# Fold weights of a routed expert layer: half of each expert's contraction computed before the routing is known

## The chip, the cores and the metric

One NeuronCore of a Trainium2 chip runs the whole program. The time is that of one execution on the device, in microseconds. Where several executions were timed, their median is given, with the lowest and the highest.

## The reference

Three layers follow one another on 3072 tokens of 512 features, all in float32.

```
state = gamma * state + k_t v_t^T ;  y_t = scale * q_t state        # 8 heads, 4 x 768 steps
e = argmax(y @ w_gate);  x = gate * eom * (relu(y @ w1[e]) @ w2[e])  # 8 experts, F = 1024
logits = x @ phi                                                    # 32 slots, 4 for each of 8 experts
d = softmax(logits, over tokens);  slot_in = d.T @ x
slot_out = relu(slot_in @ v1[e]) @ v2[e]
out = softmax(logits, over slots) @ slot_out
```

The scores of the second layer need x only through `x @ phi`. So the kernel doesn't form `relu(..) @ w2 @ phi` in that order: it folds `w2[e] @ phi` (1024 x 32) once for each expert and multiplies the hidden values by that.

## The kernel before

**Attention.** 24 steps of 128 tokens, in a loop over i with the steps' order written out by hand (`ORDER`, and `ORDER_22`, `ORDER_23`, `ORDER_24` for the last ones; each word is a function of the table `step`). One 1 MB tile `raw` per step (0.75 MB for the last of each six) holds q, k and v. It is loaded on SP's queue six steps ahead into a pool of seven buffers. Every third step, `x_put` (line 610) writes the tokens of three steps to `xs` in DRAM with four transfers on SP, and `scale_put` (line 602) their scales.

**Routing.** After the last step TensorE makes the gate logits (`gate_mm`, `gate_sum`), VectorE the choice, and TensorE the counts (line 659). VectorE works out the order in which the experts are taken (`ordi`), which depends on the counts. SP then reads the first expert's number and loads its weights. `rank` and 48 small matmuls (line 686, two for each step) make the lists of tokens per expert, and GpSimd gathers the first expert's tokens from `xs` (line 704). Then every engine passes a branch (line 818) round a part for experts with too many tokens, which isn't taken with these inputs.

**Experts.** Eight experts, each with up to 448 tokens, in order of their counts, eight units of 128 hidden features each. Unit g = 8e + f makes its hidden values with 12 matmuls (`l1`, line 883, weights split into two parts by ScalarE and VectorE, `split_w`). The pieces of the expert before (`behind`) run behind the units: scores, soft maxima, slot sums. A written order places them all, and each engine takes its instructions in that order.

**The fold.** `wq_load` loads a quarter of an expert's folded matrix (512 KB, the quarters are the units q of phi), `wq_mm` makes 16 matmuls of 128x256 (four for each q, into four groups of 32 partitions; each is two records in the profile), and `wq_turn` turns the result for use as weights in `logits`. Expert 0's four quarters are loaded as two 1 MB transfers in the routing (line 679), multiplied behind the list matmuls, and turned at line 718, ahead of the branch. For expert e + 1 the fold runs in expert e, at unit 2 (unit 4 in expert 0), and the quarters of expert e + 2 are loaded behind it.

**The last stage.** The slots go through the last experts (`moe2` weights, 32 MB in 128 tiles of 256 KB). `load_m2` loads 42 of these tiles into a pool of their own during the expert loop, and others into buffers that the loop no longer uses.

## Time and profile before

| | |
|---|---|
| median of 3 runs | 437.55 us (435.31 to 442.07) |
| the profiled execution | 435.42 us, its span 433.6 us |
| TensorE, VectorE, ScalarE, GpSimd busy | 87%, 60%, 37%, 25% of the span |
| TensorE's granted clock, mean | 0.948 of full speed |
| moved by DMA | 130.88 MB, 302 GB/s over the span |

The span runs from the first instruction of the profile to the last; the execution's time is 1.8 us longer. Attention takes the span to about 108 us, the routing to about 138, the eight experts to about 376, and the last stage the rest. Busy shares over the whole span mix these stages.

### The profile page before, as it was taken

How to read it: one execution, taken by the hardware profiler on the slowest of the kernel's cores; microseconds unless marked ns; L12 is line 12 of the kernel's file. 1: busy time of each engine (PE TensorE's matmuls, PEld its weight loads, DVE VectorE, ACT ScalarE, POOL GpSimd, SP SyncE). 2: the span in 40 equal slices, each digit the busy share in tenths (PEclk: the TensorE clock that was granted, in tenths of full speed). 3: DMA queues.
4: the chain of work that ended last, by engine and by line, in shares of the span. 5: the costliest groups of instructions: out<-in, count | busy, mean ns of one | idle time of the engine just before them, and what ended most of it. 6: DMA issues, size and time to landing. Idle time of an engine off the chain costs nothing.

```text
span 433.6 us, 11468 instructions
## 1 busy us (share of the span) xinstructions
PE 377.8 (87%) x4398; PEld 285.2 (66%) x4398; DVE 258.4 (60%) x676; ACT 162.2 (37%) x359; POOL 108.1 (25%) x117
## 2 busy tenths in 40 slices
PE   2989999998335999999999999999999996799990
PEld 2877777786214897778777867877778873224560
DVE  1498889998604365595574765754766756424350
ACT  1432222222012644655454644635454431112242
POOL 2303333321120413143052241421521212020020
PEclk9999999999655999999999999999999999699996
DMA  8999999963587798988978979889577789999998
GB/s 268 381 425 347 288 322 322 324 162 76 119 304 247 238 360 300 381 273 295 390 248 303 380 267 346 298 275 377 166 253 278 257 281 289 390 384 408 397 365 291
DMA packets 66275, 130.88 MB, mean 302 GB/s; under 512 B 10436, under 2 KB 28866, under 8 KB 63650
## 3 DMA queue, kind: packets, MB, share of 16 engines
q1 hardware_dynamic: 59426, 118.07, 78.4%
q0 software_dynamic: 3344, 8.34, 6.3%
q10 hardware_dynamic: 3440, 3.63, 2.5%
q8 instruction: 37, 0.61, 0.6%
q14 instruction: 28, 0.23, 0.2%
HBM read 116.84 MB, written 13.20 MB: 300 GB/s over the span
## 4 chain that ended last, share of the span: by engine, by line
PE 72%; DVE 9%; DMA 7%; issue 4%; ACT 3%; another core or an unknown queue 2%; SPq 1%; ACTq 1%; POOL 0%; DVEq 0%; POOLq 0%
PE hps L883 31%; PE s L414 5%; PE gps L992 5%; PE o L447 4%; PE fh L1176 4%; PE so L1213 3%; PE wps L241 3%; DMA raw<-in_qt_dram 3%; DMA xg<-xs,xidx 3%; PE lps L909 3%; PE xps L861 2%; PE o L438 2%; PE slo L1014 2%; PE st L461 1%
## 5 line engine op out<-in xcount | busy, mean ns | idle before, releaser
L883 PE MATMUL hps<-xh,wh 128*128 128x416 f32 (+2 forms) x256 | 92.0, 360 | 0.1
L883 PE MATMUL hps<-xl,wh 128*128 128x416 f32 (+2 forms) x256 | 88.9, 347 | 0.0
L883 PE MATMUL hps<-xh,wl 128*128 128x416 f32 (+2 forms) x256 | 88.7, 346 | 0.0
L222 DVE TENSOR_TENSOR wl<-r,wh 128x512 fp32r<-128x512 f32 x64 | 43.3, 677 | 43.6 <-ACT wh L221 41.2
L888 ACT ACTIVATE h<-hps 128x416 f32<-128x416 f32 (+2 forms) x64 | 32.7, 511 | 81.6 <-PE hps L883 75.9
L883 PEld LDWEIGHTS hps<-xh,wh 128*128 128x128 f32 x256 | 48.1, 188 | 15.1 <-issue 11.4
L975 POOL DMA_INDIRECT ctok<-ce,xidx x29 | 29.2, 1009 | 99.9 <-DVE ce L972 93.5
L221 ACT ACTIVATE wh<-r 128x512 fp32r<-128x512 f32 x64 | 40.0, 628 | 26.4 <-DMA r<-in_moe_w_dram 13.4
L883 PEld LDWEIGHTS hps<-xl,wh 128*128 128x128 f32 x256 | 48.2, 188 | 0.9 <-DVE xl L871 0.3
L883 PEld LDWEIGHTS hps<-xh,wl 128*128 128x128 f32 x256 | 48.1, 188 | 0.6
L704 POOL DMA_INDIRECT xg<-xs,xidx x29 | 29.9, 1031 | 65.3 <-ACT h L888 42.1
L424 DVE TENSOR_TENSOR sS<-s,csa 128x512 f32<-128x512 f32 x48 | 30.5, 675 | 16.3 <-PE s L414 16.3
L414 PE MATMUL s<-raw 64*128 64x128 f32 x384 | 32.5, 305 | 8.7 <-DMA raw<-in_qt_dram 8.3
L414 PEld LDWEIGHTS s<-raw 64*128 64x128 f32 x384 | 27.1, 204 | 11.5 <-DMA raw<-in_qt_dram 5.5
L895 DVE STREAM_TRANSPOSE hB<-h 128x416 f32<-128x416 f32 (+2 forms) x64 | 34.4, 576 | 0.0
L447 PE MATMUL o<-sS,raw 128*64 128x128 f32 x384 | 27.5, 288 | 0.0
L396 POOL TENSOR_TENSOR k<-raw,cs 128x512 f32<-128x512 f32 x20 | 22.3, 1132 | 17.0 <-DMA raw<-in_qt_dram 14.7
L479 ACT COPY xT<-o 128x512 f32<-128x512 f32 x24 | 13.9, 580 | 32.9 <-PE o L447 32.9
L241 PE MATMUL wps<-wt,phi 128*32 128x256 f32 x256 | 17.4, 414 | 9.0 <-DMA wt<-in_moe_w_dram 7.2
L447 PEld LDWEIGHTS o<-sS,raw 128*64 128x64 f32 x384 | 21.6, 142 | 3.9 <-issue 3.6
L992 PE MATMUL gps<-hB,pd 32*32 32x256 f32 x816 | 20.1, 405 | 3.7 <-DVE pd L946 3.7
L870 ACT ACTIVATE xh<-xps 128x416 fp32r<-128x416 f32 (+2 forms) x32 | 16.0, 513 | 14.8 <-DMA wt<-in_moe_w_dram 8.4
(174 smaller groups left out, 525.2 us busy)
## 6 DMA issues: line engine op xcount, KB each, us to landing
m<-in_moe_w_dram SPq DMA_DIRECT2D x41, 512.0 KB
r<-in_moe_w_dram SPq DMA_DIRECT2D x64, 256.0 KB
w<-in_moe_w_dram SPq DMA_DIRECT2D x64, 256.0 KB
wt<-in_moe_w_dram SPq DMA_DIRECT2D x28, 512.0 KB
m<-in_moe_w_dram SPq DMA_DIRECT2D x36, 256.0 KB
xs<-xr SPq DMA_DIRECT2D x32, 192.0 KB
raw<-in_kt_dram SPq DMA_DIRECT2D x5, 1024.0 KB
raw<-in_kn_dram SPq DMA_DIRECT2D x5, 1024.0 KB
```

Of the source, the lines that this page charges most:

```text
L221: nc.scalar.activation(out=hi, in_=t, func=ACTF.Copy)
L222: nc.vector.tensor_tensor(out=lo, in0=t, in1=hi, op=ALU.subtract)
L241: nc.tensor.matmul(out=wacc[k][32 * g:32 * g + 32, :], lhsT=phi[:, q, :], rhs=t, start=(q == 0), stop=(q == KD - 1), skip_group_check=True)
L414: nc.tensor.matmul(out=ps[h][:, p, :], lhsT=kq(i, p, 0)[r], rhs=kq(i, p, 1)[r], start=True, stop=True, tile_position=(64 * h, 0), skip_gro ...
L424: nc.vector.tensor_tensor(out=sS[i][:, h], in0=sps.pop((i, h)), in1=con("dm", 128)[:, 4 * h:4 * h + 4, :], op=ALU.mult)
L447: nc.tensor.matmul(out=o_at(i, p, h), lhsT=vals(i, 2 * p + h), rhs=s[:, h, p, :], start=(i % NCH == 0 and n < 4), stop=True, skip_group_ch ...
L704: gets.setdefault(e, []).append(nc.gpsimd.indirect_dma_start(out=t[0:r, :], out_offset=None, in_=xs[:, :], in_offset=bass.IndirectOffsetOn ...
L883: nc.tensor.matmul(out=ps, lhsT=a[:, kk * 128:(kk + 1) * 128], rhs=x[e][kk][:, 0:c], start=(n == 0), stop=(n == 11))
L888: relu.append(nc.scalar.activation(out=hs[g][:, 0:c], in_=ps, func=ACTF.Relu))
L895: nc.vector.transpose(out=hB[e][:, 0:NB[e], f, :], in_=hs[e * KF + f][:, 0:c].rearrange("p (b t) -> p b t", t=32))
L975: put = nc.gpsimd.indirect_dma_start(out=ctok[:, :], out_offset=bass.IndirectOffsetOnAxis(ap=xidx[0:r, e, j:j + 1], axis=0), in_=cn[0:r, j ...
L992: nc.tensor.matmul(out=ps[a][32 * j:32 * j + 32, :], lhsT=pd[q, b, :], rhs=hB[e][q, b].rearrange("p f t -> p (f t)"), start=(i == 0), stop ...
```

## The change

The contraction over the 512 features is cut in two. The units q = 0 and 1 of **all** experts, in the experts' own numbering, are loaded in the last eight steps of the attention loop (`first_load`, 1 MB each, into the pool of the attention tiles, which gets an eighth buffer). Their matmuls (`first_mm`, eight for each expert) stand in the last steps' order (P0 to P3) and between the list matmuls (4 to 7). ScalarE copies each result to SBUF (`first_copy`, four buffers), and SP stores it in a new DRAM tensor `wps` (`first_put`, 128 KB each).

The units q = 2 and 3 are still loaded by the experts' order, multiplied in the expert loop, and now for expert 0 too (at its unit 2). VectorE adds the stored half (`wq_add`), which SP has loaded by the expert's number (`part_load`), and `wq_turn` follows, for expert e at unit 1 of expert e itself (unit 2 in expert 0). Expert 1's second half is multiplied at unit 6 of expert 0, the others' at unit 3 of the expert before. The pool of the fold's quarters has two buffers in place of four, and 46 moe2 tiles in place of 42 are loaded into their own pool, with four in place of eight in the quarters' pool.

```diff
--- before.py
+++ after.py
@@ -34,15 +34,15 @@
 DX = DM + 16
 CX, NBX = max(C), max(NB)
 CAP = NT + 256
-NPRE, NX = 42, 4
+NPRE, NX = 46, 4
 NH = 6
-IO, UMM = 6, 2
+IO, UMM, QA = 6, 2, 2
 GROUPS = [(t, 3) for t in range(0, NTILE, 3)]
 ENDS = {t + n - 1: (t, n) for t, n in GROUPS}
 ORDER = "xe sc s m g1 gc xr rr g2 G0 Gb q oq os st G1 rk k".split()
 ORDER_22 = "xe sc s m st q oq os xr rr".split()
-ORDER_23 = "sc xe oq os rk3 xr".split()
-ORDER_24 = "xe g1 gc xr g2 G0".split()
+ORDER_23 = "sc xe oq os P0 rk3 xr".split()
+ORDER_24 = "xe g1 P1 C0 gc C1 xr g2 P2 P3 G0 C2".split()
 DH = (slice(0, 256), slice(256, 512))
 ORDC = "p 00 01 02 03 t 04 05 06 07 c s 10 11 o0-4 12 o4-8 13 o8-12 14 15 o12-16 16 17 d o16-20 S o20-24".split()
 QS = ((lambda nc: nc.sync, lambda nc: nc.scalar, lambda nc: nc.gpsimd), (lambda nc: nc.sync, lambda nc: nc.scalar))
@@ -165,6 +165,7 @@
 
     xs = dr.tile([NT + 1, DX], F32, name="xs")
     ctok = dr.tile([NT, NS], F32, name="ctok")
+    wps = dr.tile([E, 128, 256], F32, name="wps")
     inv = dr.tile([E * CAP, 1], I32, name="inv")
 
     phi = cst.tile([128, KD, NS], F32, name="phi")
@@ -225,7 +226,8 @@
 
 
 
-    wtt, wacc, wp = {}, {}, {}
+
+    wtt, wacc, wp, parts = {}, {}, {}, {}
 
     def wq_load(k, q, n, pool, tag):
         t = pool.tile([128, n * FF], F32, tag=tag, name="wt")
@@ -236,14 +238,17 @@
 
     def wq_mm(k, pool, tag):
         wacc[k] = pool.tile([128, 256], F32, tag=tag, name="wps")
-        for q in range(KD):
+        for q in range(QA, KD):
             for g, t in enumerate(wtt.pop((k, q))):
                 nc.tensor.matmul(out=wacc[k][32 * g:32 * g + 32, :], lhsT=phi[:, q, :], rhs=t,
-                                 start=(q == 0), stop=(q == KD - 1), skip_group_check=True)
+                                 start=(q == QA), stop=(q == KD - 1), skip_group_check=True)
+
+    def wq_add(k):
+        nc.vector.tensor_tensor(out=parts[k], in0=wacc.pop(k), in1=parts[k], op=ALU.add)
 
     def wq_turn(k, out):
         wp[k] = out
-        nc.vector.transpose(out=out, in_=wacc.pop(k).rearrange("p (f t) -> p f t", t=32))
+        nc.vector.transpose(out=out, in_=parts.pop(k).rearrange("p (f t) -> p f t", t=32))
 
 
 
@@ -311,7 +316,7 @@
 
     with ExitStack() as pa:
         sc2 = pa.enter_context(tc.tile_pool(name="sc2", bufs=2))
-        io = pa.enter_context(tc.tile_pool(name="io", bufs=IO + 1))
+        io = pa.enter_context(tc.tile_pool(name="io", bufs=IO + 2))
         one = pa.enter_context(tc.tile_pool(name="one", bufs=1))
         pT = pa.enter_context(tc.tile_pool(name="pT", bufs=1, space=PSUM))
 
@@ -381,6 +386,30 @@
                     r = slice(r.start, min(r.stop, 3 * DM))
                 nc.sync.dma_start(out=raw[i][:, r], in_=data[b][c][:, r])
 
+        ft, facc, fsum = {}, {}, {}
+
+        def first_load(e):
+            if 0 <= e < E:
+                ft[e] = io.tile([128, 4 * DM], F32, tag="raw", name="wt2")
+                nc.sync.dma_start(out=ft[e], in_=moe_w2[1, e, :, 0:QA * FF])
+
+        def first_mm(e):
+            t = ft.pop(e)
+            facc[e] = pT.tile([128, 256], F32, tag="st" if e % 2 else "w", name="fps")
+            for q in range(QA):
+                for g in range(4):
+                    nc.tensor.matmul(out=facc[e][32 * g:32 * g + 32, :], lhsT=phi[:, q, :],
+                                     rhs=t[:, q * FF + g * 256:q * FF + g * 256 + 256],
+                                     start=(q == 0), stop=(q == QA - 1), skip_group_check=True)
+
+        def first_copy(e):
+            fsum[e] = sc2.tile([128, 256], F32, tag="ws", name="ws", bufs=4)
+            nc.scalar.copy(out=fsum[e], in_=facc.pop(e))
+
+        def first_put(*es):
+            for e in es:
+                nc.sync.dma_start(out=wps[e], in_=fsum.pop(e))
+
         def kq(i, p, which):
             o = (p // 2) * DM + which * 256 + (p % 2) * 128
             return raw[i][:, o:o + 128]
@@ -620,6 +649,7 @@
             "g2": lambda i: gate_sum(i - 1), "G0": lambda i: gate_pick(i - 1), "Gb": lambda i: gate_own(i - 1),
             "G1": lambda i: gate_scale(i - 1),
             "oq": out_state, "q": lambda i: q_scale(i + 1), "os": out_scores, "st": state,
+            **{f"P{e}": lambda i, e=e: first_mm(e) for e in range(E)}, **{f"C{e}": lambda i, e=e: first_copy(e) for e in range(E)},
             "rk": lambda i: rank(i - 2), "k": lambda i: k_scale(i + 2),
         }
 
@@ -639,6 +669,7 @@
             if i < NTILE:
                 x_put(i - 3)
                 scale_put(i - 3)
+            first_load(i + IO + 1 - NTILE)
             for n in {NTILE - 2: ORDER_22, NTILE - 1: ORDER_23, NTILE: ORDER_24}.get(i, ORDER):
                 step[n](i)
             decay_table(i + 2)
@@ -651,6 +682,8 @@
         i = NTILE - 1
         x_put(i)
         gate_own(i)
+        first_copy(3)
+        first_put(0, 1, 2, 3)
         cp = pT.tile([128, 512], F32, tag="s", name="cp", bufs=2)
         key, counts = cp[:, 0:E], cp[:, E:2 * E]
         for o, w, b, first, final in ((key, eights, base[:, 0, 0:E], True, False), (key, ones, base[:, 1, 0:E], False, False),
@@ -676,15 +709,19 @@
         load_er(0)
         for g in range(3):
             load_w(g)
-        for q in range(0, KD, 2):
-            wq_load(0, q, 2, io, "raw")
         rank(i)
         lp = pT.tile([128, 32], F32, tag="s", name="lp", bufs=2)
         nc.tensor.matmul(out=lp, lhsT=ones, rhs=base[:, 2, :], start=True, stop=False)
         for u in range(NTILE):
             for a in range(2):
                 nc.tensor.matmul(out=lp, lhsT=lrow[:, u, :], rhs=lcol[:, u, a, :], start=False, stop=(a == 1 and u == NTILE - 1))
-        wq_mm(0, pT, "w")
+            if u == NTILE - 4:
+                for e in (4, 5, 6):
+                    first_mm(e)
+                    first_copy(e)
+        first_mm(7)
+        first_copy(7)
+        first_put(4, 5, 6, 7)
         lx = one.tile([128, E, 4, E], F32, name="lx")
 
         def lists(r):
@@ -715,7 +752,6 @@
         nc.vector.tensor_reduce(out=lim[:, E:E + 1], in_=lim[:, 0:E], axis=AX.X, op=ALU.max)
         nc.vector.tensor_copy(out=limi, in_=lim)
         lists(slice(1, E))
-        wq_turn(0, pd[:, 0:KF, :])
 
     whl = ctx.enter_context(tc.tile_pool(name="whl", bufs=3))
 
@@ -836,7 +872,7 @@
     hp = ctx.enter_context(tc.tile_pool(name="hp", bufs=NH))
     hbp = ctx.enter_context(tc.tile_pool(name="hbp", bufs=1))
     w2p = ctx.enter_context(tc.tile_pool(name="w2p", bufs=8))
-    wup = ctx.enter_context(tc.tile_pool(name="wup", bufs=KD))
+    wup = ctx.enter_context(tc.tile_pool(name="wup", bufs=KD - QA))
     with ExitStack() as pb:
         sp = pb.enter_context(tc.tile_pool(name="sp", bufs=1))
         ps_h = pb.enter_context(tc.tile_pool(name="ps_h", bufs=2, space=PSUM))
@@ -893,6 +929,10 @@
             if f == 0:
                 hB[e] = hbp.tile([128, NBX, KF, 32], F32, tag="hB", name="hB")
             nc.vector.transpose(out=hB[e][:, 0:NB[e], f, :], in_=hs[e * KF + f][:, 0:c].rearrange("p (b t) -> p b t", t=32))
+
+        def part_load(k):
+            parts[k] = sp.tile([128, 256], F32, tag="wpp", name="wpp")
+            nc.sync.dma_start(out=parts[k], in_=wps[bass.ds(er[k], 1)].rearrange("o p n -> (o p) n"))
 
         def load_w2(e, fs, pool=w2p, tag="w2"):
             for f in fs:
@@ -1046,11 +1086,12 @@
                 load_w2(e, (2 * f - 6, 2 * f - 5))
 
         load_er(1)
-        for q in range(KD):
-
-            get = wq_load(1, q, 1, wup, "wu")
-            if q == 0:
+        for q in range(QA, KD):
+
+            get = wq_load(0, q, 1, wup, "wu")
+            if q == QA:
                 after(get, gets[0])
+        part_load(0)
         for j in range(len(XT[0])):
             if j == 1:
                 split_w(0)
@@ -1091,15 +1132,25 @@
             else:
                 l1(g)
             behind(e - 1, f)
-            u = UMM if e else UMM + 2
-            if f == u and e + 1 < E:
-                wq_mm(e + 1, ps_1, "A")
-                wq_turn(e + 1, sp.tile([128, KF, NS], F32, tag="wp", name="wp", bufs=2))
-            if f > u and f <= u + 3 and e + 2 < E:
-
-                for q in ((0, 1), (2,), (3,))[f - u - 1]:
+
+
+            if g == UMM:
+                wq_mm(0, ps_1, "A")
+                wq_add(0)
+            if f == (1 if e else UMM):
+                wq_turn(e, sp.tile([128, KF, NS], F32, tag="wp", name="wp"))
+            if e + 1 < E:
+                if f == (2 if e else 3):
+                    part_load(e + 1)
+                if e == 0 and f in (3, 4):
+                    wq_load(1, QA + f - 3, 1, wup, "wu")
+                if f == (3 if e else 6):
+                    wq_mm(e + 1, ps_1, "A")
+                    wq_add(e + 1)
+            if e + 2 < E and f in ((4, 5) if e else (7,)):
+                for q in (QA + f - 4,) if e else range(QA, KD):
                     wq_load(e + 2, q, 1, wup, "wu")
-            elif G - 14 < g < G - 6 and f % 2:
+            elif g in (G - 12, G - 11):
                 load_m2(wup, "wu", 2)
             if g == G - 6:
                 load_w2(e, range(4), xp, "xy")
```

## Rows read from the trace of the kernel before

**Rows 1.** The page, chain that ended last, shares of the span by line.

```profile
PE hps L883 31%; PE s L414 5%; PE gps L992 5%; PE o L447 4%; PE fh L1176 4%; PE so L1213 3%; PE wps L241 3%; DMA raw<-in_qt_dram 3%; DMA xg<-xs,xidx 3%; PE lps L909 3%; PE xps L861 2%; PE o L438 2%; PE slo L1014 2%; PE st L461 1%
```

**Rows 2.** Busy time in two expert periods: stretch, engines, PEclk, DMA share, GB/s.

```profile
198.96:228.92 29.96, 29.66 (x303) 23.16 (x306) 19.00 (x44) 15.02 (x31) 9.68 (x9) 1.00 0.91 315
228.92:258.82 29.90, 29.55 (x294) 23.07 (x298) 18.87 (x44) 14.98 (x31) 9.67 (x9) 1.00 0.88 314
```

**Rows 3.** The chain in order of time: start us, us, what.

```profile
118.24 11.44 DMA xg<-xs,xidx
...
138.16 11.22 PE hps L883 x60
149.38 1.86 PE wps L241 x32
...
230.78 4.68 PE hps L883 x24
...
318.20 1.86 PE wps L241 x32
```

**Rows 4.** Timeline, attention's end and routing: start us, us, engine, line, operation.

```profile
79.86 1.09 PE L447 MATMUL o<-sS,raw 128*64 128x128 f32 x16
...
100.29 1.09 PE L447 MATMUL o<-sS,raw 128*64 128x128 f32 x16
...
103.72 0.37 ACT L467 COPY sts<-st 128x256 f32<-128x256 f32 x1 [0.92 <-PE st L461]
...
106.53 1.09 PE L447 MATMUL o<-sS,raw 128*64 128x128 f32 x16
...
108.31 0.85 PE L497 MATMUL g<-xT,wg 128*32 128x384 f32 x8 [0.68 <-ACT xT L479]
109.03 2.60 SPq L610 DMA_DIRECT2D xs<-xr  x4
...
109.76 0.84 PE L512 MATMUL g<-csa,gsb 128*128 128x16 f32 x6 [0.60 <-ACT gsb L505]
...
112.39 0.17 PE L659 MATMUL cp<-run,eights 128*128 128x8 bf16 x1 [1.75 <-DVE run L538]
...
116.89 0.60 PE L686 MATMUL lp<-lcol,lrow 128*128 128x32 bf16 x6 [2.93 <-DVE lrow L595]
...
118.24 1.27 POOL L704 DMA_INDIRECT xg<-xs,xidx  x1 [1.10 <-DVE sq L711]
...
121.16 1.01 POOL L704 DMA_INDIRECT xg<-xs,xidx  x1 [0.30 <-issue]
...
125.91 0.63 ACT L221 ACTIVATE wh<-r 128x512 fp32r<-128x512 f32 x1 [13.03 <-POOLq L818]
...
128.38 1.94 PE L241 MATMUL wps<-wt,phi 128*32 128x256 f32 x16 [1.72 <-SPq L818]
...
130.38 0.45 DVE L246 STREAM_TRANSPOSE pd<-wps 128x256 f32<-128x256 f32 x1 [10.58 <-PE wps L241]
...
134.56 0.49 DVE L852 TENSOR_SCALAR xg<-xg 128x512 f32<-128x512 f32 x1 [3.72 <-DVEq L818]
...
135.30 2.79 PE L861 MATMUL xps<-cs,xg 128*128 128x128 f32 x12 [4.99 <-DVE xg L852]
```

**Rows 5.** Busy time in the attention loop and in short stretches of the routing.

```profile
40.00:50.00 10.00, 9.36 (x182) 8.18 (x182) 9.54 (x30) 2.93 (x8) 3.40 (x4) 1.00 0.97 320
...
94.00:96.00 2.00, 2.00 (x50) 1.72 (x48) 1.93 (x6) 0.15 (x1) 1.16 (x3) 1.00 0.03 8
110.00:112.00 2.00, 0.64 (x8) 0.57 (x8) 1.08 (x7) 0.22 (x1) 0.00 (x0) 0.93 0.92 171
112.00:114.00 2.00, 1.57 (x52) 1.46 (x51) 1.76 (x10) 0.20 (x1) 0.00 (x0) 0.50 0.93 216
122.00:124.00 2.00, 0.00 (x0) 0.00 (x0) 0.00 (x0) 0.00 (x0) 0.17 (x1) 0.50 1.02 421
```

**Rows 6.** Busy time in the last stage.

```profile
396.00:420.00 24.00, 23.01 (x318) 14.33 (x319) 10.08 (x32) 7.47 (x18) 2.26 (x3) 1.00 1.04 391
```

## The prediction

> **What bounds the kernel now.** I read the chain of waits first, then the busy time stage by stage, then the routing stretch instruction by instruction, and last the transfers in two-microsecond windows. The chain by line [rows 1] puts 31% of the span on the expert layer's matmuls and 3% on the fold matmuls (`wps`, moe_w2 times phi). In the expert loop TensorE has no slack: 29.66 of 29.96 us busy in one expert, 29.55 of 29.90 in the next [rows 2]. What leaves TensorE's program there leaves the time. An expert's fold is 32 records in 1.86 us on the chain, and the chain has seven of them, from 149.38 to 318.20 [rows 3].
>
> The routing stretch, from the last attention step (107.6) to the first expert matmul (138.16), is bound by waits. The token gather is issued at 118.24 and the chain gives it 11.44 us [rows 3], beside 2.75 MB that SP issues around it (lines 677 to 680). But the gather isn't what ends last. The two 1 MB fold loads make the fold's second half run at 128.38; VectorE is held by its transpose until 130.38 + 0.45; only then does VectorE pass the branch of line 818, which costs 3.72 us, and scale the gathered rows at 134.56; the transposes run at 135.30 and the first expert matmul at 138.16 [rows 3, 4]. ScalarE had passed at 125.91, 3.74 us after GpSimd's third gather issue ended (121.16 + 1.01) [rows 4].
>
> **The loop's sum.** Before: 7 folds x 1.86 = 13.0 us of TensorE on the chain (expert 0's is in the routing). After: eight half folds in the loop, 16 records each, 0.93, so 7.4. Gain 5.6. Each half needs one VectorE add of 128x256 out of PSUM. No row shows such an add; the transpose of the same PSUM tile, 0.45 us [rows 4], is nearest, and I take that. Its bounds are nothing (hidden under the next unit of expert matmuls, 4.68 us for two [rows 3]) and 8 x 0.45 = 3.6 exposed. It is hidden for experts 2 to 7, where a whole unit of expert matmuls lies between the fold and the next user of PSUM tag A. It is not for expert 1: its fold stands at the end of unit 6 of expert 0, and the next thing on TensorE is the transposes of expert 1 into the same tag. That costs 0.45 plus the hand-over, 0.6 once. The 128 KB part loads queue on SP behind a VectorE transpose of the step before; the weight loads behind them have two units (4 us) in hand, so I price them at nothing; if that cover failed, a unit's start would slip by the transfer. The loop moves 5 MB less (7 MB of fold weights out, 1 MB of parts and 1 MB more of moe2 in), so DMA, at 0.88 to 0.91 there [rows 2], doesn't become the limit. Loop gain 5.6 - 0.6 = **5.0** (3.5 to 5.6).
>
> **The attention loop's end.** The new loads take the slots of attention tiles as these come free: first load after the score product at 79.86, last after the one at 106.53, eight in all, so about 81.4 to 107.6, the last three from 101.4 on [rows 4]. TensorE gets P0 ahead of the gate product at 108.31, P1 ahead of the sum at 109.76, P2 and P3 ahead of the counts at 112.39 [rows 4]. Each half fold is 0.93 at full clock and 1.94 at the lower one (the row at 128.38 is just half a fold). The gaps there are waits on ScalarE and VectorE and swallow most: P0 moves the gate product by 0.3, P1 the sum by 0.65, P2 and P3 end 0.15 after the counts could start. In all 0.8 us. Copies to SBUF cost ScalarE 0.37 each [rows 4]; it is idle.
>
> **The routing's sum.** Removed: the 2 MB of fold loads beside the gather, the fold of expert 0 and its transpose ahead of the branch. In their place comes a ladder of waits that I take for the new limit. The copies go to four buffers, so the copy of expert 4 waits until the store of expert 0's part has *landed*; the fold of expert 6 waits for that copy (same PSUM bank), and it stands on TensorE ahead of the last six list matmuls (116.89), on which the gather's indices rest. SP issues that store right behind the token write of line 610 (109.03 to 111.63), and this stands behind the new loads.
>
> When does it land? I take it that the write waits out the loads ahead of it. 1 MB at 421 GB/s (122 to 124) is 2.5 us; a token write alone kept the queue busy 0.92 and 0.93 of two windows, 3.7 us [rows 5]. From 81.4 to 107.6, 26.2 us, come 8 x 2.5 + 3 x 3.7 = 31.1 us of work: 5 us of backlog, and 2 more since the last three loads come within 6 us. So the last token write ends near 107.6 + 7 + 3.7 = 118.3, and the store near 119. Least: no backlog, 115, since in the run before that write was over by 114 [rows 5]. Most: 122, if mixed loads and writes go at the loop's own 320 GB/s [rows 5]. Before, the queue had idle time in this stretch (0.03 in use at 94 to 96 [rows 5]), so nothing but these transfers stands in it.
>
> From 119: copy 0.37, half fold 0.93 (1.94 at the lower clock), list matmuls 0.60, two small VectorE operations and GpSimd's start 1.0: the gather is issued near **122.5**, 4.3 later than now. Its third issue ends 3.9 later, 126.4; GpSimd's branch 3.74, 130.2; weight split 0.63 and, estimated from that, row scaling 0.6 on ScalarE, 131.5; two thirds of the transposes (2.79), 133.4; first expert matmul **133.5**. VectorE no longer waits for a fold and has passed its branch long before. That is 138.16 - 133.5 = **4.6** gained (8.4 with the store at 115, 1.7 with 122).
>
> SP is late as well: it must store parts 4 to 7, the last after expert 7's fold, before it can branch, so the next expert weight and expert 0's other two units are issued near 131 to 134. With 2.5 us for 1 MB they are there by 136.5, and they are needed three units of 2.24 (11.22 for five [rows 3]) after 133.5, at 140.2. Covered, by 3.7 us; without that cover expert 0 waits by as much as they are late.
>
> The clock was at its lower level (0.50) from 112 on [rows 5] until the expert matmuls were under way, and stays so across the gather's wait in both kernels, since TensorE is idle in it in both. I count no gain there.
>
> *What a page says of the order.* The token write of the run before went into a queue that was empty (0.03 of its time in use at 94 to 96), so its 3.7 us [rows 5] don't show in what order it and a load would go. The Trainium skill (DMA: Bandwidth & Descriptors, section "Queues, rings and completion order") says that a DMA engine takes the descriptors of one issuing engine in ring order, and takes turns between issuers. By that SP's token write waits out SP's loads, as summed above; if it took turns with them, the store would land near 115 to 116 and the time would be near 422.
>
> **The end.** moe2 weights preloaded: 42 + 8 tiles before, 46 + 4 after. The last stage runs DMA at 1.04 and TensorE 23.01 of 24 us [rows 6]; its loads start when the loop lets its buffers go, so the stage moves as a whole. Nothing.
>
> **Sum.** The profiled execution is 435.42 (span 433.6). 435.42 - 4.6 - 5.0 = 425.8. The median of the three runs shown is 437.55, the lowest 435.31: the profiled one is among the fast ones, and I forecast for that kind: **426**.
>
> **Rivals.**
> 1. *The queue keeps up.* The token write isn't held, the store lands by 115 or 116, and the gather goes out near 119. For it: idle queue time after 94. Against: 31 us of work in 26. Gain 8.4 + 5.0: **422**.
> 2. *The ladder eats the routing gain.* Store at 122 or later, lower clock for the folds in the routing, SP late behind its stores: first expert matmul at 136.5 to 138.5, and only the loop's gain is left: **430 to 431**.
> 3. *Slower.* The same ladder, with the store landing so late that the loop's 5.0 are eaten: the first expert matmul has to start after 143.2, so the store to land after about 129. That asks for 10 us more of backlog than I sum, for instance loads at 250 GB/s and token writes at 6 us each. For it: the two-microsecond windows vary. Against: the middle of the attention loop carries as much per step now, at 0.97 of the queue [rows 5]. Price: **437**, up to 440.
> 4. *It doesn't do what it says.* The half folds leave TensorE's program but it waits as long for VectorE's adds or the part loads: no loop gain, routing as summed: **430**.
>
> **How the numbers follow.** Forecast (424 to 428) 0.45, the first rival 0.20, the second 0.25, the third 0.07, the fourth 0.03. The range goes from below the first (420) to above the second and fourth (434); it leaves out the third and some of the ends. About 2% is what a measurement of this kernel can tell from no change, 428.8 against the median, 426.7 against the profiled time. The first rival and two thirds or so of the forecast lie under it: faster 0.52, same 0.43, slower 0.05.
>
> **What would show it.** Right: in the loop, `wps` records in groups of 16 at 0.93 us and a period near 29.0 us per expert in place of 29.9; no fold between the list matmuls and the transposes that ends after 127; first expert matmul between 132 and 135; the fold of expert 6 preceded by idle time that ends with ScalarE's copy, and that copy by a DMA. Queue share near 1 from 82 to 119. Wrong: the gather issued before 120 (the ladder isn't there), or the first expert matmul held by something else (SP's late weights, VectorE's branch); a longer expert period, with TensorE waiting for VectorE at the adds; or a different last stage.

## The result, and the profile after

The changed kernel takes 432.38 us (median of 20 runs, 429.62 to 435.51), the kernel before 438.78 beside it (20 runs, 434.90 to 443.81): ratio 0.987, interval 0.985 to 0.989. That is 6.4 us less; 426 was forecast, in a range of 420 to 434. The profiled execution of after took 433.64 us, span 431.9.

Stage by stage. Before was profiled twice and after three times (this profile, and two runs below). Rows are means in us, cut at the first instruction of each kind on TensorE; the profiles of one kernel differ by up to 3.9 in the second row and 2.0 in the fourth, so a difference of less than 1 us is a hint only:

| stretch | before | after | change | predicted |
|---|---|---|---|---|
| start to gate product | 107.5 | 108.3 | +0.9 | +0.3 |
| gate product to first expert matmul | 31.8 (29.85, 33.71) | 26.7 (27.50, 25.91, 26.68) | -5.1 | -4.9 |
| first expert matmul to transposes of expert 1 | 18.4 | 19.9 | +1.5 | +0.6 |
| transposes of expert 1 to those of expert 7 | 176.6 | 172.8 | -3.8 | -5.6 |
| from there to the last stage | 45.9 | 46.7 | +0.8 | 0 |
| last stage | 55.3 | 55.3 | 0 | 0 |

The routing gained what was forecast, the loop didn't: its three rows together give 1.5 where 5.0 stood.

The routing of after, from the timeline (the rows that answer to [rows 4]): start us, us, engine, line, operation, and in brackets the idle time before and what ended it.

```profile
109.25 0.83 PE L526 MATMUL g<-xT,wg 128*32 128x384 f32 x8
...
111.63 4.87 SPq L639 DMA_DIRECT2D xs<-xr  x4
...
116.60 4.09 SPq L411 DMA_DIRECT2D wps<-ws  x4
...
123.29 0.70 ACT L407 COPY ws<-fps 128x256 f32<-128x256 f32 x2 [9.03 <-DMA wps<-ws]
...
123.71 1.93 PE L401 MATMUL fps<-wt,phi 128*32 128x256 f32 x16 [6.82 <-DMA wps<-ws]
...
125.58 0.34 PE L717 MATMUL lp<-lcol,lrow 128*128 128x32 bf16 x6
...
126.66 1.27 POOL L741 DMA_INDIRECT xg<-xs,xidx  x1 [8.34 <-DMA wps<-ws]
...
129.58 1.01 POOL L741 DMA_INDIRECT xg<-xs,xidx  x1 [0.30 <-issue]
...
133.14 0.49 DVE L888 TENSOR_SCALAR xg<-xg 128x512 f32<-128x512 f32 x1 [4.91 <-DVEq L854]
...
133.89 2.79 PE L897 MATMUL xps<-cs,xg 128*128 128x128 f32 x12 [6.23 <-DVE xg L888]
...
136.75 0.69 PE L919 MATMUL hps<-xh,wh 128*128 128x384 f32 x1
```

Read upwards from the gather at 126.66: its index needs the list matmuls (125.58), which stand behind a fold (123.71), which waits for ScalarE's copy (123.29), which had been idle for 9.03 us until a *store* landed. That is the ladder. The store was issued behind the token write (111.63) and landed near 123.2. On the other side, 7.2 us lie between gather issue and transposes, against 17.06 before [rows 4]. SP in a view is the engine that the text calls SyncE from here on.

The windows of after show the queue full where that was expected, and then the clock. Columns: stretch, length, PE, PEld, DVE, ACT, POOL busy, granted clock, DMA share, GB/s.

```profile
82.00:90.00 8.00, 7.40 (x118) 5.92 (x114) 6.67 (x19) 1.99 (x5) 4.12 (x5) 1.00 1.02 329
90.00:100.00 10.00, 9.13 (x167) 7.43 (x162) 9.69 (x27) 3.18 (x8) 3.58 (x4) 1.00 0.99 300
100.00:110.00 10.00, 9.55 (x184) 7.55 (x187) 8.21 (x28) 3.09 (x8) 1.12 (x2) 1.00 1.00 343
110.00:118.00 8.00, 6.89 (x144) 4.32 (x136) 5.39 (x28) 1.91 (x6) 0.65 (x1) 1.00 0.97 317
...
122.00:126.00 4.00, 2.29 (x26) 0.98 (x30) 0.04 (x1) 0.94 (x3) 0.00 (x0) 0.50 0.78 220
...
213.87:242.93 29.06, 28.91 (x278) 22.49 (x275) 18.99 (x44) 14.66 (x32) 9.65 (x9) 1.00 0.82 283
```

The share is 0.97 to 1.02 from 82 to 118, at 300 to 343 GB/s. The clock, at its lower level from 112 on before [rows 5], is now at full level until 118; TensorE, which has folds there, is busy 6.89 of the last 8 us. From 122 to 126, behind an idle stretch, it is at the lower level (0.50). The expert of the last line (against [rows 2]) takes 29.06 us in place of 29.9; the middle six together take 3.8 less, 0.64 each, so one period told too little.

One expert on the chain of after (answer to [rows 3]): start us, us, what.

```profile
231.00 1.00 PE wps L243 x16
232.00 2.44 PE hps L919 x12
...
243.00 1.82 PE xps L897 x16
244.82 2.46 PE hps L919 x12
247.30 0.45 PE hps L919
247.75 0.37 issue
248.12 2.34 PE hps L919 x11
```

The half fold is 1.00 (0.93 was taken). The second unit of the expert, one matmul, a hole, then eleven, is new: before, two units ran through in 4.68 to 4.72. What comes ahead of the hole, from the timeline:

```profile
246.21 0.63 ACT L222 ACTIVATE wh<-r 128x512 fp32r<-128x512 f32 x1 [3.22 <-DMA r<-in_moe_w_dram]
246.75 1.72 ACT L906 ACTIVATE xh<-xps 128x416 fp32r<-128x416 f32 x4
247.48 2.07 DVE L907 TENSOR_TENSOR xl<-xps,xh 128x416 fp32r<-128x416 f32 x4
248.12 0.46 PE L919 MATMUL hps<-xl,wh 128*128 128x416 f32 x1 [0.37 <-issue]
```

ScalarE waits 3.22 us for a weight tile. Its split of the expert's tokens (xh), VectorE's (xl) and the second unit's matmuls follow from there. The waits of after name what holds the loads (waiter, what it waits for: us in total, times, longest), over the span and from 136 to 362; the last line is the second one's counterpart before, over the span:

```profile
SPq L935 <- DVE wp L251: 37.0, 7, 6.3
```

```profile
ACT wh L222 <- DMA r<-in_moe_w_dram: 32.8, 21, 3.5
```

```profile
ACT wh L221 <- DMA r<-in_moe_w_dram: 13.4, 11, 1.9
```

SyncE stands 5.3 us per expert at the part load (line 935), because the part has one buffer and VectorE still has to transpose the last one out of it. The weight loads of line 213 stand behind it, and ScalarE's split of those weights comes late.

### The profile page after: what moved, and what is told of

Read it like the earlier page. It is cut to its first block, busy times and chain, and to the rows that moved or that the text cites. A ratio compares the mean times of both kernels' runs of the same rounds, so it can differ in the third digit from the quotient of the medians.

```text
span 431.9 us, 11518 instructions
## 1 busy us (share of the span) xinstructions
PE 380.4 (88%) x4398; PEld 283.8 (66%) x4398; DVE 259.7 (60%) x684; ACT 164.0 (38%) x367; POOL 107.4 (25%) x117
## 4 chain that ended last, share of the span: by engine, by line
PE 52%; DMA 8%; ACT 3%; DVE 2%; issue 2%; ACTq 1%; SPq 0%; DVEq 0%
PE hps L919 28%; DMA r<-in_moe_w_dram 6%; PE fh L1227 4%; PE slo L1054 4%; PE gps L1032 4%; PE so L1264 3%; PE lps L949 3%; PE xps L897 2%; DMA w<-in_moe_w_dram 2%; PE wps L243 1%; PE gsum L1045 1%; PE lsum L970 1%; ACT ot L1324 1%; PE ops L1322 1%; ACTq L1325 1%
## 5 line engine op out<-in xcount | busy, mean ns | idle before, releaser
L443 PE MATMUL s<-raw 64*128 64x128 f32 x384 | 31.1, 298 | 10.1 <-DMA raw<-in_qt_dram 10.1
L443 PEld LDWEIGHTS s<-raw 64*128 64x128 f32 x384 | 25.9, 198 | 12.6 <-DMA raw<-in_qt_dram 6.2
L897 PE MATMUL xps<-cs,xg 128*128 128x128 f32 (+2 forms) x116 | 15.6, 284 | 7.3 <-DVE xg L888 6.2
L897 PEld LDWEIGHTS xps<-cs,xg 128*128 128x128 f32 (+2 forms) x116 | 12.9, 148 | 12.2 <-ACTq L854 7.0
```

The source lines that it names most:

```text
L443: nc.tensor.matmul(out=ps[h][:, p, :], lhsT=kq(i, p, 0)[r], rhs=kq(i, p, 1)[r], start=True, stop=True, tile_position=(64 * h, 0), skip_gro ...
L897: nc.tensor.transpose(out=ps[kk][:, j * 128:j * 128 + r], in_=xg[e][j][0:r, kk * 128:(kk + 1) * 128], identity=ident[0:r, 0:r])
```

## The experiments

The times behind an experiment are its median in us, and the ratio to the kernel before on the same chip. Before's own median lies between 435.4 and 440.0 on the four chips, so runs of different chips are compared by ratio or by stage. "Loop" is first expert matmul to last stage, "middle" the transposes of expert 1 to those of expert 7.

**Both kernels again** (no edit).

> The kernel before once more, for the same reason: its one profile (435.42) lies 3.4 us under the median of its 20 runs (438.78). If the difference is in the routing, the first expert matmul starts at 140 or later in place of 138.16; if it is in the expert loop, an expert's period is longer than 29.9 us. Ratio 1.00.

> The changed kernel once more, to see which of its stages vary from run to run. If the ladder of waits in the routing is a property of the order (my reading of its first profile), the gather is issued between 125 and 128 again and the first expert matmul starts between 135.5 and 138. If that profile was an unlucky run, as its 433.64 us beside a median of 432.38 could mean, the gather is issued earlier by 2 us or more and the time is near 430. Ratio to the kernel before 0.985 to 0.99 by both.

438.66 (0.998, 0.995 to 1.002) and 430.77 (0.982, 0.978 to 0.985). Before's routing varies: its first profile, on which I forecast, had 17.06 us from gather to transposes, this one has 20.90:

```profile
116.60 1.27 POOL L704 DMA_INDIRECT xg<-xs,xidx  x1 [1.10 <-DVE sq L711]
...
137.50 2.79 PE L861 MATMUL xps<-cs,xg 128*128 128x128 f32 x12 [6.04 <-DVE xg L852]
```

The profile of 435.42 lay 3.4 us under the median of before, and I had not allowed for that.

**Is it the ladder?**

```diff
-  fsum[e] = sc2.tile([128, 256], F32, tag="ws", name="ws", bufs=4)
+  fsum[e] = sc2.tile([128, 256], F32, tag="ws", name="ws", bufs=8)
```

> The changed kernel with eight buffers in place of four for the copies of the first halves. Theory of the ladder: the copy of expert 4 no longer waits for a landed store, so the list matmuls end near 118.5 and the gather waits only for the scales' write, which SP issues behind four stores at 120.8: gather near 123.3, first expert matmul near 133.5, 3.3 us less than the changed kernel, ratio to the kernel before 0.979 to 0.981. Rival, the queue alone: the token write itself lands so late behind the loads that the gather couldn't have started before 126; then nothing moves, ratio 0.986 to 0.988.

430.33 (0.981, 0.978 to 0.985). Timeline of that run:

```profile
117.13 0.58 PE L717 MATMUL lp<-lcol,lrow 128*128 128x32 bf16 x6 [0.32 <-DVE lrow L624]
...
122.85 1.27 POOL L741 DMA_INDIRECT xg<-xs,xidx  x1 [5.46 <-DMA r<-in_moe_w_dram]
```

The lists are done 6 us earlier than in its neighbour, the changed kernel again (117.71 against 123.69), but the gather goes out only 1.6 us earlier (124.44 there). With the ladder gone, the gather waits for something that lands at 122.8; I take it to be the tokens and scales that it reads, written behind the loads. (The releaser that the profile names has nothing to do with the gather; it is what landed just then.) The 3.3 us that I expected didn't come: the medians differ by 0.4.

**Scales ahead of the parts:** the edit above, and the stores of parts 0 to 3 moved behind the scale write and three weight loads.

```diff
-        first_put(0, 1, 2, 3)
...
-        first_put(4, 5, 6, 7)
+        first_put(*range(E))
```

> The changed kernel with eight copy buffers and all eight stores of the first halves moved behind the scales' write and the first three expert weights on SP. With eight buffers alone the list matmuls ended at 117.7 but the gather went out at 122.85 only, since the scales' write stands behind four stores. Theory, that the stores ahead of the scales' write are now the limit: gather near 119.5, first expert matmul 2 to 3 us earlier than with eight buffers (133.2), ratio to the kernel before 0.974 to 0.977. Rival, that the token write itself lands at 121 or later behind the loads: gather at 122 or later and the same time as with eight buffers, ratio 0.981.

429.76 (0.989, 0.981 to 0.997). The scale write is issued at 114.77, 3.5 us earlier than in the run above, and the gather goes out at 122.58, as there. So it isn't the scale write's place behind the parts.

**The loads' bytes:** 128 KB in place of 1 MB each; the half folds leave out the other seven eighths.

```diff
-                nc.sync.dma_start(out=ft[e], in_=moe_w2[1, e, :, 0:QA * FF])
+                nc.sync.dma_start(out=ft[e][:, 0:256], in_=moe_w2[1, e, :, 0:256])
```

> The changed kernel with first loads of 128 KB in place of 1 MB, whose 256 columns all eight first matmuls use (leaves out seven eighths of the first halves' data). It takes the load's bytes out of SP's queue and leaves the order, the stores, the ladder and the loop. Theory of the queue (the loads delay token write and stores): the store of expert 0's part lands near 115, the gather goes out at 119 to 120 in place of 124.4 to 126.7, first expert matmul at 127 to 130, ratio 0.965 to 0.972. Rival, the ladder's own latency (a store's time to land, copy, fold at the lower clock) without the loads: gather at 123 or later, ratio 0.978 to 0.982.

425.42 (0.980, 0.969 to 0.991).

```profile
117.14 1.27 POOL L741 DMA_INDIRECT xg<-xs,xidx  x1 [1.13 <-DVE sq L748]
...
125.07 0.49 DVE L888 TENSOR_SCALAR xg<-xg 128x512 f32<-128x512 f32 x1 [6.36 <-DVEq L854]
```

The gather waits for nothing but its index, 5.4 us before the run above. 7 MB of loads hold the writes back by about that much, and with that the gather. On this chip the time is 4.3 us under the run above, which has other edits too (eight buffers, late stores); about that is what the change would give more if the queue kept up (rival 1).

**The loads alone, in the kernel before:** the eight loads into eight buffers, used by nothing.

```diff
+        def first_load(e):
+            if 0 <= e < E:
+                t = io.tile([128, 4 * DM], F32, tag="raw", name="wt2")
+                nc.sync.dma_start(out=t, in_=moe_w2[1, e, :, 0:2 * FF])
```

> The kernel before with the eight 1 MB loads in the last steps of the attention loop and its eighth buffer, and nothing that uses them: the whole fold as it was. The price of the bytes by itself. Queue theory: the token write lands at 121 to 122 in place of 115, the gather goes out at 121 to 123 in place of 116.6 to 120, first expert matmul 3 to 5 us later than before, ratio 1.007 to 1.012. Rival, that the loads only hurt through the stores and the ladder: gather as before, ratio 0.998 to 1.002.

435.42 (1.005, 1.002 to 1.009).

```profile
121.71 1.27 POOL L710 DMA_INDIRECT xg<-xs,xidx  x1 [6.06 <-DMA r<-in_moe_w_dram]
...
130.51 0.45 DVE L246 STREAM_TRANSPOSE pd<-wps 128x256 f32<-128x256 f32 x1 [12.21 <-PE wps L241]
...
134.99 0.49 DVE L858 TENSOR_SCALAR xg<-xg 128x512 f32<-128x512 f32 x1 [4.03 <-DVEq L824]
```

The gather is issued 5.1 us later than in the second profile of before (116.60), and the rows are scaled at 134.99 against 136.75 there and 134.56 in [rows 4]. In these profiles a late gather doesn't move the rows: expert 0's fold, its transpose and the branch (4.03) end last. The ratio still puts the loads' price at 0.2 to 0.9%, which these rows don't place.

**The other side of that:** the kernel before with expert 0's two fold loads issued in steps 20 and 21, by a fixed expert number in place of the one in the register.

```diff
+            if i in (20, 21):
+                wq_load(0, 2 * (i - 20), 2, io, "raw")
...
-        for q in range(0, KD, 2):
-            wq_load(0, q, 2, io, "raw")
```

> The kernel before with the two fold loads of expert 0 taken out of the routing: they fetch a fixed expert's matrix in steps 20 and 21 of the attention loop (so expert 0 gets a fold that isn't its own). Fold and transpose stay where they are. It shows what the routing owes to those 2 MB alone. Theory, as in the prediction (fold, transpose and branch are the chain, the gather rides behind the same 2 MB): VectorE passes its branch near 124, the gather lands by 123 to 125, first expert matmul at 127 to 130 in place of 138.2 to 140.4: 9 to 12 us less, ratio 0.972 to 0.979. Rival, the gather's own landing and the branches hold the transposes: first expert matmul at 134 or later, ratio 0.99 or above.

424.98 (0.978, 0.968 to 0.988): by the ratio some 9.5 us less, from 2 MB out of the way, as expected.

```profile
117.75 1.27 POOL L704 DMA_INDIRECT xg<-xs,xidx  x1 [1.10 <-DVE sq L711]
...
120.64 0.45 DVE L246 STREAM_TRANSPOSE pd<-wps 128x256 f32<-128x256 f32 x1 [1.32 <-PE wps L241]
...
125.06 0.49 DVE L852 TENSOR_SCALAR xg<-xg 128x512 f32<-128x512 f32 x1 [3.98 <-DVEq L818]
```

The fold's transpose comes almost 10 us earlier, the rows are scaled 9.5 us earlier than in [rows 4] with a gather issued half a microsecond earlier. The routing of before was bound as the prediction read it.

**The loop's sum alone:** the kernel before with q = 2 and 3 only, in the folds of experts 1 to 7.

```diff
-        for q in range(KD):
+        lo = 2 if k else 0
+        for q in range(lo, KD):
...
```

> The kernel before with only the units q = 2 and 3 loaded and multiplied for experts 1 to 7 (leaves out the first halves, nothing in their place; expert 0 whole). It is the loop's gain without its price: no parts, adds, stores or new order. Theory of the prediction (what leaves TensorE's program leaves the time): 7 x 0.86 = 6.0 us less between the first expert matmul (138 to 140) and the last stage, ratio 0.985 to 0.988. Rival, that another engine's chain is nearly as long as TensorE's, so that part of it comes back as waits: an expert period above 29.2 in place of 29.0 and a ratio of 0.990 or more.

429.73 (0.988, 0.981 to 0.996). Middle 168.34. The run above, with whole folds and on the same chip, has 174.48, and the one with the loads alone 174.08: 5.7 to 6.1 us for six half folds.

**Two buffers for the part:**

```diff
-NPRE, NX = 46, 4
+NPRE, NX = 44, 4
...
-  parts[k] = sp.tile([128, 256], F32, tag="wpp", name="wpp")
+  parts[k] = sp.tile([128, 256], F32, tag="wpp", name="wpp", bufs=2)
```

> The changed kernel with two buffers for the loaded parts, so that SP's load of the next part no longer waits for VectorE's transpose of the part before (37 us of waiting on SP in the profile); to make room, 44 moe2 tiles are preloaded in place of 46. Theory of SP's head of line: the expert weights come in time again, ScalarE's wait for them falls from 32.8 us to near the 13 of the kernel before, the stall of 0.4 to 1 us in the second unit of an expert goes, the expert period falls from 29.3 to near 28.9, and the time by 2.5 to 4 us: ratio 0.978 to 0.982. Rival, VectorE's adds and the new place of the transposes hold TensorE: the wait on SP goes, the stall stays, ratio 0.986 to 0.988.

431.43 (0.984, 0.980 to 0.987). Its waits from 160 to 330:

```profile
PEld lsum L970 <- DVE ll L957: 3.4, 5, 0.9
...
ACT wh L222 <- DMA r<-in_moe_w_dram: 2.6, 5, 1.1
...
PE lsum L970 <- DVE ll L957: 1.8, 4, 0.6
```

In the second profile of after the same window has 29.2 us of late weights; here 2.6, and SyncE waits for no transpose any more. The hole in the second unit is gone. But a wait ahead of the log sum comes in, the middle is 172.2, 0.6 under the mean of after, and the time, which was to fall by 2.5 to 4 us, is no better than that of the changed kernel on the same chip (430.77). Both profiles of before have this wait, here the first:

```profile
PE lsum L930 <- DVE ll L917: 1.9, 4, 1.0
```

In the middle TensorE waits there 1.9 and 1.8 us before, 0, 0 and 0.4 in the three profiles of after, 2.1 with two buffers. In these profiles, where late weights hold TensorE at the start of an expert, it doesn't wait here; with the weights in time, it does. So this run alone didn't settle the loop, and three more took it apart.

**No part load, and neither part load nor add:** in the first a constant is added in the place of the part, in the second the transpose reads PSUM.

```diff
-            nc.sync.dma_start(out=parts[k], in_=wps[bass.ds(er[k], 1)]...)
-        nc.vector.tensor_tensor(out=parts[k], in0=wacc.pop(k), in1=parts[k], op=ALU.add)
+        nc.vector.tensor_tensor(out=parts[k], in0=wacc.pop(k), in1=con("col")[:, 0:256], op=ALU.add)
```

> The changed kernel with two buffers for the part and no part load: VectorE adds a constant table to the fold in its place, so the parts don't reach the sums. If the part loads' place in SyncE's program costs what the loop lacks, an expert takes 28.5 us and the time is 425 to 427. If VectorE's add does, or the other transfers do, it stays at 29.1 and 430 to 431.

> The changed kernel without part loads and without adds; the transpose reads the fold from PSUM, as before the change, and the parts don't reach the sums. This is the loop that my sum of 5.0 us had in mind, with the routing of the changed kernel. If parts and adds are the whole of what is missing, the loop from the first expert matmul to the last stage takes 232 to 233 us, as in the kernel of before with half the fold left out, and the time is 422 to 425. If the missing part lies in the transfers of the loop or in the clock, it stays above 236 and the time above 427.

430.09 (0.982, 0.973 to 0.991) and 430.25 (0.982, 0.973 to 0.991). Both came out on the second side of what I had written down: an expert takes 29.0, the loop more than 236, the time 430, so by these expectations parts and adds aren't all that is missing. The medians don't tell these from the changed kernel's (430.77 to 432.38); each comes from 4 runs. The profiles do: loop 236.6 and 236.4, against 239.8, 240.1 and 238.2 in the three of after; middle 171.4 and 171.5. By them the add is worth 0.2 us and the part loads about 2.8 of the loop, but each is one profile, of the fastest of its four executions. The loop of 232 to 233 was taken from the run with half folds alone, which doesn't have the wait ahead of the log sum. Here the chain still has it:

```profile
246.80 1.98 another core or an unknown queue
248.78 0.03 issue
248.81 0.75 DVE acc L1055
249.56 0.51 DVE ll L954
250.06 0.04 issue
250.11 0.45 PE lsum L967
```

It needs neither parts nor adds, and before has it. It is no part of the change. Against before, which has it too, the middle without parts is 5.1 shorter, as six half folds are (6 x 0.86 = 5.2).

**Both edits:** two buffers, and the stores behind the scales; then the same on another chip, beside the changed kernel.

> The changed kernel with both earlier edits: two buffers for the part, and eight for the sums with all stores behind the scales. If SyncE's blocked part load is what holds the second unit after the transposes, and nothing but chance brought the wait ahead of the log sum with two buffers, both are gone and an expert takes 28.5 us in place of 29.3: 425 to 427. If the wait ahead of the log sum comes with every kernel in which SyncE is not blocked, an expert stays at 29.1 and the time at 430 to 431.

> The changed kernel once more, as the neighbour of the next run: 430 to 433, and 239 to 240 from the first expert matmul to the last stage.

> The version with two buffers for the part and all stores behind the scales, once more on one chip beside the changed kernel. If the part loads held by SyncE cost the loop 2 us and the early scale write gives the routing 1.5 us more, it is 3 to 4 us under the changed kernel; if its first time was chance, within 1 us of it.

428.12 (0.977, 0.968 to 0.987), with the log-sum wait and 28.8 to 29.1 us for an expert; then 431.16 (0.985, 0.981 to 0.990) for the changed kernel and 428.77 (0.979, 0.974 to 0.983) for this one: 2.4 us by the medians where 3 to 4 were expected, six runs each, 429.30 to 432.33 against 426.88 to 430.75. Middle 171.4 and 171.2 for this version. The profiled run of the second was its slowest (430.75), so its stages aren't the ones that win. It is the best version here that computes the whole result; the intervals against before still touch those of after, and these runs don't tell how much of the 2.4 is the second buffer's.

**Writes on another queue** (the last token write and scale write on ScalarE, with the stores late; then with two buffers; then with one phi unit preloaded in place of two).

```diff
-        x_put(i)
+        x_put(i, nc.scalar)
...
-        scale_put(i)
+        scale_put(i, nc.scalar)
```

> The kernel of e3_order (eight copy buffers, stores behind the scales' write) with the last token write and the last scales' write issued by ScalarE, on its own queue, in place of SP. In e3_order the list was ready at 117.1 and the gather went out at 122.6, after a token write that SP issued from 110.5 on. Theory, that the write waits out SP's loads ahead of it: from another issuer it lands by 117 to 118, the gather goes out at 118 to 119.5, first expert matmul near 129 to 131, 2 to 4 us less than e3_order. Rival, that the DMA engines as a whole are behind (8 MB and the writes), whoever issues: gather at 121.5 or later again and no difference. ScalarE's four issues may delay the last gates by 1 to 2 us.

> e7_actq with two buffers for the loaded parts and 44 preloaded moe2 tiles. If the two repairs lie in different stages they add: expert period 29.1, no wait of ScalarE for expert weights, and in expert 0 the add of expert 1's half no longer waits behind a late weight (transposes of expert 1 held 0.6 in place of 1.7). 1 to 2 us less than e7_actq; ratio to the kernel before 0.965 to 0.973. If the waits only change places, as the period of 29.07 beside 29.17 in e2_part2 hints, no difference to e7_actq.

> e8_all with one unit of four in place of two done ahead of the routing (512 KB loads, four first matmuls for each expert, three quarters of the fold in the loop, three buffers for it and 42 preloaded moe2 tiles). Half the bytes in the queue and half the routing's matmuls, against 8 x 0.46 us more in the loop. Queue theory: the gather goes out 1 to 2 us earlier than in e8_all and the loop is 3.5 us longer, so the time is 1 to 3 us above e8_all. Rival, that the bytes cost more than the matmuls give back: at or below e8_all.

438.9 (1.014, 1.007 to 1.021), 437.9 (1.007, 1.004 to 1.011), 440.4 (1.017, 1.010 to 1.024). Slower than before, and not for a reason that I had put down. Waits of SyncE in the first of them from 85 to 130, and the window in which it stands:

```profile
SPq L394 <- DMA xs<-xr: 15.7, 2, 15.4
```

```profile
104.00:110.00 6.00, 5.55 (x97) 3.63 (x92) 3.71 (x10) 2.39 (x5) 1.12 (x2) 1.00 0.00 0
```

One of SyncE's loads waits 15.4 us for a token write, and for 6 of them no transfer runs at all. Why the load waits for that write isn't shown. So these three don't answer what they were made for, whether writes on another issuer would pass the loads. They do add one thing: with two buffers, and in a batch where the wait ahead of the log sum is absent, the middle is 168.5, against 170.3 with one.

## Why the prediction was wrong

**The loop is the step that failed**, and in it the sentence "the weight loads behind them have two units (4 us) in hand, so I price them at nothing". The row that would have told was not looked for: VectorE's transpose, for which the part load waits, comes up to 6.3 us after SyncE gets there (37.0 us over seven experts), more than the 4 in hand. The prediction's fallback ("a unit's start would slip by the transfer") had the wrong mechanism too: it isn't the transfer of 128 KB that is waited for, but VectorE. SyncE takes its instructions in order, so a load that waits for VectorE holds all that SyncE issues behind it. This accounts for the largest piece that an edit here removes, 1.3 of the 3.5 us that are missing; the other pieces follow.

The terms, by the profiles:
- *Six half folds in the middle, 5.6:* 5.1 without part loads (before 176.6, without part loads 171.4 and 171.5), and 5.7 to 6.1 where the log-sum wait is absent (174.1 and 174.5 to 168.3). The fold's count was right; its size is 1.00, and 6 x 0.86 = 5.2.
- *Part loads, 0:* they take 1.3 of these 5.1 in after (172.8, from 171.7 to 173.7). Two buffers give back most of it in the middle: 172.2, 171.4, 171.2, and clearly so in the batches without the log-sum wait, 168.5 against 170.3, 172.1 and 174.7. The time of the second buffer alone doesn't show it (431.43 beside 430.77), since the log-sum wait takes the place of the holes.
- *Expert 0, +0.6:* +1.5. Two half folds are 2 x 1.00 on the chain where one whole was 1.86, and the transposes of expert 1 wait for VectorE's add 0.66, 1.66 and 0.55 us in the three profiles, 0.96 in the mean; the other 0.4 isn't placed. Here they are in after (a timeline shows the half fold as 1.07, the whole as 1.93):

```profile
154.29 1.07 PE L243 MATMUL wps<-wt,phi 128*32 128x256 f32 x16
...
155.55 0.42 DVE L247 TENSOR_TENSOR wpp<-wps,wpp 128x256 f32<-128x256 f32 x1
156.02 1.92 PE L897 MATMUL xps<-cs,xg 128*128 128x128 f32 x16 [0.66 <-DVE wpp L247]
```

  The add itself is 0.42 (0.45 was taken); it stands behind a weight split on VectorE.
- *After the transposes of expert 7, 0:* +0.8. It is gone without part loads (46.0, 45.8 against 45.9 before), but no part is loaded in that stretch, and two buffers don't bring it back (46.6, 47.0). What it is stays open.

Sum 1.5 for the loop where 5.0 stood.

**The routing's ladder was right, its gain in part luck.** 4.9 was forecast from gate product to expert matmul, 5.1 measured. But two errors meet there: the routing of after is 26.7 us where the sum has 24.9, and before's own is 31.8 in the mean where the profile that I forecast on has 29.85. The first expert matmul starts at 136.75, 134.40 and 133.96 (133.5 forecast).
- *The store:* it landed near 123.2 in the first profile (119 taken, 122 the upper bound). I took 421 GB/s for the loads; with writes among them the queue moved 300 to 343 from 82 to 118, nearer to the rate of the upper bound.
- *The ladder's fold:* 1.93 at the lower clock, where 0.93 was summed. The listed terms add up to 121.9 with the one and 122.9 with the other; the gather went out at 126.7, 124.4 and 123.9 (122.5).
- *From gather to expert matmul:* 10.0 to 10.1 in the three (11.0). The branch, priced on GpSimd's side, stands on VectorE's in the view (4.91).

What the ladder costs is small: without it the next wait, for the writes behind the loads, lets the gather go at 122.85, 1.0 to 3.8 us earlier than in the three.

**The rivals.** The fourth's condition (TensorE waits for VectorE's adds or the part loads, 0.03) held in part, for 1.3 us in the middle and 0.96 at expert 1. The second's (store at 122 or later, expert matmul from 136.5) held in the first profile alone; that its price, 430 to 431, is near the result is chance, since the loop that it keeps whole is what is missing.

**The level was a choice of mine, and cost as much as the loop**: the sum was made from 435.42, "among the fast ones". The median over 20 runs is 438.78, 3.4 higher. Of the 6.4 us between forecast and result, that is 3.4 and the loop 3.5; the rest (start and routing 0.4 late, the stage means 0.6 short of what the medians show) about cancels.

**SyncE covered, last stage, clock, bytes**: TensorE waits for nothing in expert 0's units; the last stage is 55.3 in both. The clock did more than nothing: at full level, half folds ahead of the ladder came in pairs in 1.93 us, the time of one at the lower level, but none of these ends last. In four of the five changed kernels whose gather goes out earlier (eight buffers, late stores, small loads, and the second one with both edits) the granted clock is still 0.50 to 0.55 in the first 4 us of expert matmuls, and the stretch up to the transposes of expert 1 takes 20.7 to 20.9 us, against 19.3 to 20.4 in after: part of an earlier start is lost again. In the bytes, the fold loads of the loop are 6 MB less, not 7 (14 MB to 8), and the moe2 tiles 50 in both; the 5 MB stand.

## What to carry to other kernels

When a DMA moves to an engine's program, look up what it waits for, not how many bytes it moves: in order behind a wait on a compute engine, 128 KB held the weight loads behind it for 5 us per expert, and a second buffer of 1 KB per partition ended that (late weights 29.2 to 2.6 us). Then look for the wait that takes its place: here the one ahead of the log sum did, and the second buffer alone moved no time. Work taken away from a stretch that ends in a ladder of waits is worth the distance to the next wait, here 1 to 4 us. And compare a single profile with the median and spread of the runs before adding to it.

## What the runs showed of the hardware that I had not expected

- In these runs a write behind loads is late with the loads. The gather, which reads the token and scale writes, goes out at 122.85 and 122.58 behind eight loads of 1 MB (eight buffers; late stores) and waits for no write past 117.1 behind eight of 128 KB. The Trainium skill (DMA: Bandwidth & Descriptors, section "Queues, rings and completion order") says that the descriptors of one issuer go in ring order; these runs agree with that, but would also agree with shared bandwidth, and the runs with the write on ScalarE don't tell.
- VectorE's idle time that the profile books to the branch varies: 3.72 and 4.78 us in the two profiles of before, 4.91 in after, 6.36 in the run with small loads. A wait for the gathered rows, which are scaled next, may be hidden in it.
- ScalarE and VectorE wait up to 3.6 us ahead of the log sum for something that the trace doesn't name, in 11 of 19 profiles, and never in the other eight, which are those of two batches (all stores behind the scales, small loads, the two edits of the kernel before that follow, the loads alone, and the three with writes on ScalarE). The kernel doesn't decide it: loops with the same code are on both sides, and so is one chip. Open.
